# Attention beside an MLP on one core: one more add ahead of the logits in every chunk, a weight load in five parts, and a new order of pieces

## The chip, the cores and the metric

The kernel runs on one core of a Trainium2 chip. The metric is the device time of one execution in microseconds (us); the time given for a kernel is the median of its runs. Besides that there is one profiled execution of each kernel, from which all rows are taken.

## The reference

The layer norm of x (2048 tokens, 640 channels, bf16) goes through two branches, and both are added to x.

```python
xn  = layernorm(x)                                  # over 640 channels
q, k, v = split(xn @ wqkv)                          # 32 heads of 20 channels
idx = pos[:, None] - 2 * arange(8)[None, :]         # 8 keys, each 2 tokens further back
logits = einsum("hsd,hswd->hsw", q, k[idx]) * 20 ** -0.5      # idx < 0: -1e9
o   = einsum("hsw,hswd->hsd", softmax(logits), v[idx])
mlp = gelu(xn @ w1 + b1) @ w2 + b2                  # 640 -> 1536 -> 640
out = x + o @ wo + mlp
```

## The kernel before

Tokens are worked through in four chunks n = 0..3 of 512, and each chunk in four blocks of 128. The 640 channels make five tiles of 128 (KT = 5), with channels arranged so that the 128 partitions of a tile hold 4 channels of each of the 32 heads. An attention window of 8 keys is too small for matrix products over heads, so VectorE (DVE) does it: for each block j and half h of the window, qk multiplies q by four shifted views of k, [128, 4, 5, 128] in one instruction (L433), into the one buffer `half`.

The sum over a head's 20 channels is taken in two steps. First pa pieces on DVE add some channel tiles into others (L465, below). What is left is summed by lg on TensorE (PE): matmuls with `head_of`, a 128 x 32 matrix of zeros and ones, 128 x 512 columns each, the four blocks going to four groups of 32 columns (L474). `KEPT[n]` says how many channel tiles are left for lg: with 2, pa..0 adds tiles 2, 3 into 0, 1 (2048 elements a partition), pa..1 adds tile 1 into 0 (1024), and lg has 2 tiles x 2 halves x 4 blocks = 16 matmuls.

```python
a, b = ((slice(0, 2), slice(2, 4)), (slice(0, 1), slice(1, 2)), (slice(0, 1), slice(4, 5)))[k]
...
ts = {KT: range(KT), 3: (0, 1, 4), 2: (0, 4), 1: (0,)}[KEPT[n]]
...
for k in range({KT: 0, 3: 1, 2: 2, 1: 3}[KEPT[n]]):
    piece(f"pa{n}{j}{k}", do_pa, n, j, k)
```

Then come the softmax (cl copies the logits out of PSUM on ScalarE, ACT; m, mx, ss, ri, at on DVE; ex on ACT), xd (a DMA spreads the weights over the partitions), av (DVE multiplies v by them, into `half` again), aa (adds the two halves; a DMA of GpSimd's queue for chunks 0 to 2, DVE for chunk 3), ab and ot (the last adds on DVE, into the single buffer oT). Since `half` is there once, the order on DVE is qk, pa of chunk 0, then of chunk 1, av of 0, av of 1, qk of 2, and so on, and each hand-over waits for an lg.

PE has the other work: projections (hj for chunk 0, by pairs of blocks; pj for the others), the MLP's first product f1 with its Gelu ge on ACT, and the output products o{n}{block}{0..3} (MLP) and o{n}{block}4 (attention, which needs ot). Products of PE go to four PSUM banks that pieces share (psA), emptied by copies on ACT (pc, hc, gc) or by ge; outputs go to one pair lo, hi of banks, emptied by oc and stored by od with an adding DMA. ACT also does part of the layer norms (su, sq, rs, xn). Transposed x comes from PE in chunk 0 (tp, copied by tc), by DMA from SP's queue later (tc). xp stores x to the output, xb adds b2.

Each engine works its instructions off in order. That order is written by hand in ORDER, one string of piece names; a piece's engine and buffers are fixed, and its waits follow from what it reads and writes.

The first pieces: x's first block is loaded on SP's queue (L130), the second on ACT's; then SP loads wq, wk, two more blocks of x, wv, four more blocks of x, w1 in two parts, and (ldx) the rest of x. ga and gb2 to gb4 multiply block 0 by wq tile by tile of the inner 640 (ga: tiles 0 and 1, gb: 2, 3, 4; L349), gd and ge block 1; hj are L380, f1 L586, pj L336, o L622 and L624.

Of the kernel before, what the change touches and what calls it, by code (L numbers as in the profile page):

```python
# [39 lines left out]
ORDER = """  # L40
wa ho st00a sum1 st00 rs00 rc00 neg1 sq1 xn00a tp00a wb xn00b tp00b mean1 tc00a rs01 rc01 tb b1 tc00b ga gb2 xn01 tp01
tc01a tc01b gb3 gb4 gd ge gc4 gc1 hj100 st02a st02 rs02 hc100 st03a st03 hj101 gc0 rc02 xn02 rs03 hj102 rc03 xn03
hc101 hc102 tp02 tc02 hj202 tp03 tc03 hj201 hc201 hj010 st11a hc010 st13a hc202 st12a hj012 hc012 hj112 hc112 f10_3
st11 ldx hj011 f10_9 st10a st10 st12 st13 rs1 qk011 ge0_3 rc1 xn13 pad01 qk000 qk001 tc13 ge0_9 xn12 tc12 pa000 qk010
pk hj110 hc110 hj111 hc111 hc011 qk030 qk031 qk021 pad11 xn11 f10_10 tc11 pa010 xn10 qk020 tc10 ge0_10 f10_2 ge0_2
hj200 hc200 f10_0 pa030 f10_6 f10_11 su20 ge0_6 xp2 su22 su23 pj111 pc111 ge0_0 su21 ng2 pj110 pc110 pj104 pc104 sq23
pj120 pc120 ge0_11 sq20 pj114 pc114 pj113 pc113 pa001 pa020 pa021 pj102 pc102 pa031 pa011 lg0 cl0 mask m0 hj212 hc212
pj123 pc123 mx0 ex0 pj103 pc103 pj112 pc112 ss0 ri0 pj101 pc101 pj100 pc100 qk110 qk100 ld2 ldo xb2 sq22 qk130 pj124
pc124 hj211 sq21 qk121 rs2 pj121 pc121 hj210 hc210 rc2 f10_8 qk131 hc211 f11_9 ge1_9 xp0 xn20 f10_1 ge0_1 f10_7 tc20
f11_5 xb0 qk120 xn21 tc21 qk101 ge1_5 ge0_7 xn23 tc23 ge0_8 xn22 qk111 o000 f11_8 ge1_8 pa130 at0 pa110 f11_0 ge1_0  # L50
pa100 pad12 f10_5 ge0_5 f11_3 ge1_3 f11_6 su32 tc22 pa120 pa101 xd00 f10_4 su33 pj214 pc214 pa111 su31 su30 pj210
pc210 pad21 xd02 ge0_4 pj211 pa121 ge1_6 pa131 lg1 pj200 pad02 av000 av001 aa00 pc200 ng3 sq32 sq31 sq30 av020 pc211
av021 xd01 av011 o001 pj213 pc213 pj122 pj202 pc202 av010 o002 ab00 ot00 pj204 pj212 o003 pc212 pj223 pj222 cl1 aa02
xd03 pc122 av030 av031 m1 mx1 sq33 rs3 pj201 rc3 pc204 o004 oc00 ab02 ot02 pj224 ex1 o020 aa01 aa03 ss1 ri1 xn33 at1
ab01 ot01 ab03 o021 o022 o023 o024 xp1 tc33 pc201 xn32 tc32 pc222 oc02 ot03 od02 f12_7 xd10 av101 pad22 xd12 pc223
f11_4 xn30 o030 o031 o032 o033 pc224 xd11 xn31 pj221 av100 aa10 o034 oc03 f11_2 o010 ge1_4 tc31 av120 o011 o012 o013
o014 av110 av111 aa11 ge2_7 pc221 od03 f11_7 ge1_7 pj203 pc203 ge1_2 xd13 f11_1 av131 tc30 pj311 pc311 av130 aa13
pj304 f12_3 ge2_3 pj310 pc310 pc304 ge1_1 pj302 av121 aa12 ab10 ot10 f11_10 pc302 ge1_10 pj313 pc313 qk201 qk200 pj312
pj314 ab11 ot11 qk210 pc312 oc01 od01 f13_8 ge3_8 qk211 o130 ab13 pa200 pc314 f11_11 ge1_11 qk231 f12_6 o131 ot13
qk230 xb3 f12_0 ge2_0 pj220 pc220 o132 o133 o134 oc13 pj301 pc301 pa210 ge2_6 ab12 ot12 qk221 pj300 pj324 pc300 qk220  # L60
f13_7 xb1 pc324 od13 pa211 pj303 o120 pa230 pa220 pa231 pc303 pad31 pa221 pa201 lg2 ge3_7 cl2 qk301 f12_2 m2 mx2 ex2
f13_10 f12_8 ge2_8 o121 o122 o123 od00 o124 oc12 qk310 ss2 pj320 pc320 qk311 ri2 at2 xd22 xd20 o110 o111 qk331 o112
o113 o114 oc11 od11 qk330 f13_6 ge3_6 f12_5 ge2_5 ge3_10 o100 ge2_2 qk320 pa330 qk321 pa320 f13_5 f12_4 ge3_5 pj322
f13_2 o101 ge2_4 qk300 xd21 pc322 pa321 o102 o103 o104 ge3_2 pa300 pa301 pa331 pa310 pa311 lg3 f13_3 av210 f13_9 oc10
od10 od12 av211 aa21 ge3_3 f12_10 ge2_10 xd23 av230 av200 f12_1 ge2_1 ge3_9 av231 aa23 f12_9 ge2_9 f13_1 ge3_1 f13_4
f12_11 av201 av221 ab21 ge3_4 av220 pj321 o210 o211 o212 f13_0 ot21 ge2_11 o213 o214 f13_11 cl3 m3 mx3 ex3 pad32 ss3
ri3 at3 xd32 oc21 o200 o201 pc321 o202 aa20 ab20 ot20 ab23 ot23 ge3_0 aa22 o203 o310 o204 oc20 pj323 pc323 ab22 ot22
av320 o230 o231 o232 o233 o234 od20 oc23 av321 aa32 xd30 o311 o312 od21 ab32 o220 o221 o222 o223 o224 ge3_11 xd31
av311 od23 o313 av301 av310 oc22 od22 o320 o321 o322 o323 av300 ot32 o324 oc32 aa31 ab31 ot31 o314 oc31 o300 o301 o302
xd33 od32 aa30 o330 o303 ab30 ot30 o304 av331 av330 aa33 ab33 o331 o332 o333 ot33 od31 xl o334 oclo oc30 ohi ochi ochd  # L70
od30
""".split()


# [713 lines left out]
```

## Time and profile before

| | us |
|---|---|
| runs | 206.86, 207.37, 207.10; median 207.1 |
| profiled execution, own time | 207.49 |
| its span in the profile | 205.7 |
| PE busy | 200.8 |
| DVE busy | 175.4 |
| ACT busy | 127.7 |

The granted clock is 1.0. A row of the profile names the source line, the engine, the operation, what it writes and reads, the shape, how often it ran, its busy time and its mean. A row of a timeline begins with the start and the length of a merged run of equal instructions; in square brackets stands how long the engine was idle ahead of it and what ended that. The chain of waits lists, in order of time, the work that ended last, followed back from the end. Neighbouring instructions overlap by some 0.1 us on DVE and by more on PE, so what an instruction costs in a run is the distance to the next start, not its length.

### The profile page before, as it was taken

What the parts mean: (1) busy time and instruction counts of PE and PEld (TensorE: products, weight loads), DVE (VectorE), ACT (ScalarE), POOL (GpSimd) and SP (SyncE); (2) the same over time, 40 slices, a digit from 0 to 9 for tenths busy, and PEclk for the clock granted to TensorE, in tenths of its full rate; (3) what the DMA queues carried; (4) which work ended last, traced back from release to release, by engine and by line L of the source; (5) the groups of instructions that cost most, each with busy time, mean ns of one, the idle gap of its engine ahead of it and who ended that gap; (6) DMA issues with size and microseconds to landing.
All of it is one profiled execution on the core that took longest, in us unless ns stands there. A gap on an engine that the chain in (4) does not pass through costs nothing.

```text
span 205.7 us, 3262 instructions
## 1 busy us (share of the span) xinstructions
PE 200.8 (98%) x1285; PEld 112.2 (55%) x1285; DVE 175.4 (85%) x214; ACT 127.7 (62%) x242; POOL 34.4 (17%) x49
## 2 busy tenths in 40 slices
PE   7899999999999999999999999999999999999994
PEld 2797745565445555555555554555444555555552
DVE  3489999379998989949999994999979979799981
ACT  5488999899999879916466344834616854221210
POOL 2000000050000422102703303001023420311210
DMA  6999389969258599899996965018209998931244
GB/s 210 390 397 370 75 232 326 403 102 185 64 116 264 99 186 181 142 192 124 207 198 113 144 107 64 0 16 182 41 0 132 162 193 162 192 41 17 30 52 64
DMA packets 27335, 31.77 MB, mean 154 GB/s; under 512 B 9272, under 2 KB 22072, under 8 KB 27320
## 3 DMA queue, kind: packets, MB, share of 16 engines
q0 software_dynamic: 7408, 12.78, 39.4%
q1 hardware_dynamic: 19600, 18.58, 31.4%
q8 instruction: 10, 0.16, 0.3%
q10 hardware_dynamic: 312, 0.20, 0.3%
q14 instruction: 5, 0.04, 0.1%
HBM read 10.00 MB, written 7.54 MB: 85 GB/s over the span
## 4 chain that ended last, share of the span: by engine, by line
PE 95%; DMA 3%; SPq 0%; DVE 0%; issue 0%
PE lo L622 29%; PE hps L586 25%; PE pps L336 24%; PE hi L624 7%; PE gps L380 7%; DMA wq_sb<-in_A_wqkv_dram 3%; PE L L474 2%; PE gps L349 1%; PE tp L280 0%; SPq L130 0%; DVE osb L652 0%
## 5 line engine op out<-in xcount | busy, mean ns | idle before, releaser
L586 PE MATMUL hps<-xnT,w_sb 128*128 128x512 bf16 x240 | 55.6, 379 | 0.0
L433 DVE TENSOR_TENSOR half<-qT,kT 128x2560 bf16<-128x2560 bf16 x32 | 46.2, 1482 | 2.9 <-PE L L474 2.8
L622 PE MATMUL lo<-w_sb,hT 128*128 128x512 bf16 x144 | 41.3, 379 | 0.0
L586 PEld LDWEIGHTS <-w_sb 128*128 128x128 bf16 x240 | 22.9, 98 | 26.3 <-issue 0.8
L629 ACT CAST osb<-lo 128x512 bf16<-128x512 f32 x15 | 8.8, 587 | 36.8 <-PE hi L624 18.5
L624 PE MATMUL hi<-w_sb,hT 128*128 128x128 bf16 x144 | 31.5, 219 | 0.0
L602 ACT ACTIVATE hT<-hps,b1T 128x512 bf16<-128x512 f32 x36 | 24.0, 683 | 10.7 <-PE hps L586 10.7
L465 DVE TENSOR_TENSOR half<-half 128x2048 bf16<-128x2048 bf16 (+1 forms) x32 | 29.0, 952 | 0.2
L635 POOL DMA_DIRECT2D out_dram<-osb x15 | 13.6, 973 | 77.1 <-ACT osb L630 68.5
L557 DVE TENSOR_TENSOR half<-vT,x_sb 128x2560 bf16<-128x2560 bf16 x16 | 22.8, 1485 | 4.4 <-DMA x_sb<-e 3.0
L557 DVE TENSOR_TENSOR half<-vT,ax 128x2560 bf16<-128x2560 bf16 x16 | 22.8, 1485 | 2.3 <-PE L L474 1.4
L622 PEld LDWEIGHTS <-hT 128*128 128x128 bf16 x144 | 14.1, 98 | 16.8
L622 PE MATMUL lo<-wo,oT 128*128 128x512 bf16 x80 | 23.1, 379 | 0.0
L567 POOL DMA_DIRECT2D half<-half x12 | 14.3, 1195 | 48.9 <-DVE half L557 48.5
L336 PE MATMUL pps<-xnT,wv_sb 128*128 128x512 bf16 x75 | 18.5, 379 | 0.0
L336 PE MATMUL pps<-xnT,wq_sb 128*128 128x512 bf16 x75 | 18.3, 379 | 0.0
L336 PE MATMUL pps<-xnT,wk_sb 128*128 128x512 bf16 x75 | 17.7, 379 | 0.0
L624 PE MATMUL hi<-wo,oT 128*128 128x128 bf16 x80 | 16.9, 219 | 0.0
L173 ACT ACT_TABLE_LOAD x12 | 15.4, 1283 | 0.9 <-PEq L772 0.7
L624 PEld LDWEIGHTS <-hT 128*128 128x128 bf16 x144 | 14.1, 98 | 2.2
L573 DVE TENSOR_TENSOR half<-half 128x1280 bf16<-128x1280 bf16 x16 | 13.1, 820 | 1.3 <-DMA half<-half 1.2
L622 PEld LDWEIGHTS <-oT 128*128 128x128 bf16 x80 | 7.8, 98 | 9.4
(91 smaller groups left out, 263.7 us busy)
## 6 DMA issues: line engine op xcount, KB each, us to landing
half<-half POOLq DMA_DIRECT2D x12, 640.0 KB, 7.1
w_sb<-in_B_w_dram SPq DMA_DIRECT2D x4, 960.0 KB, 11.0
out_dram<-osb POOLq DMA_DIRECT2D x15, 160.0 KB, 4.0
ax<-e SPq DMA_DIRECT2D x8, 256.0 KB, 4.8
x_sb<-e SPq DMA_DIRECT2D x8, 256.0 KB, 4.8
out_dram<-b2bc POOLq DMA_DIRECT2D x3, 640.0 KB, 8.7
x_sb<-in_A_x_dram SPq DMA_DIRECT2D x1, 1280.0 KB, 12.9
out_dram<-x_sb SPq DMA_DIRECT2D x2, 640.0 KB, 8.7
```

The lines of the kernel that those rows point to most:

```text
L173: nc.scalar.activation(warm[:], nc.const_aps.tensor(0.0, [P, 1], F32), func)
L336: nc.tensor.matmul(ps[:], lhsT=wqkv_p[which][:, ti, to, :], rhs=xnT[:, ti, :], start=(ti == 0), stop=(ti == KT - 1),)
L380: nc.tensor.matmul(ps[:, to - a, :], lhsT=wqkv_p[which][:, ti, to, :], rhs=tiles["xnT", 0][:, ti, pair * 2 * P : (pair + 1) * 2 * P], star ...
L433: nc.vector.tensor_tensor(out=half[:, j, h], in0=q[:, :, at].unsqueeze(1).to_broadcast([P, W // 2, KT, P]), in1=window(k, h, at), op=ALU.mult,
L465: nc.vector.tensor_tensor(out=kept, in0=kept, in1=gone, op=ALU.add)
L557: nc.vector.tensor_tensor(out=half[:, j, h], in0=window(qkv_tile(n, 2), h, cs), in1=ax_view(n)[:, j, ws, :].unsqueeze(2).to_broadcast([P, ...
L567: nc.gpsimd.dma_start(a, b, accum_op=ALU.add, max_dma_last_dim=CUT)
L586: nc.tensor.matmul(ps[:], lhsT=w1_sb[:, ti, ft * P : (ft + 1) * P], rhs=tiles["xnT", n][:, ti, :], start=(ti == 0), stop=(ti == KT - 1),)
L602: nc.scalar.activation(hT, tiles["hps", n, ft][:], ACT.Gelu_apprx_tanh, bias=b1T[:, ft : ft + 1], scale=1.0)
L622: nc.tensor.matmul(lo[:], lhsT=lhs, rhs=rhs[:, 0:CH], start=first, stop=last)
L624: nc.tensor.matmul(hi[:, 0 : D - CH], lhsT=lhs, rhs=rhs[:, CH:D], start=first, stop=last)
L635: nc.gpsimd.dma_start(rows, tiles["osb", n, bl][:], accum_op=ALU.add)
```

## The change

`KEPT` is 1 for all chunks. So each block has a third add, pa..2, of tile 4 into tile 0 (16 more instructions on DVE, 1024 elements a partition), and each lg has 8 matmuls, over tile 0 alone (32 fewer in all). wq comes in five DMAs, one for each tile of the inner dimension, 160 KB each, in place of one of 800 KB. ORDER is new throughout. The core of the diff, with a part of the two orders:

```diff
-KEPT = (2, 2, 2, 2)
+KEPT = (1, 1, 1, 1)
...
-wa ho st00a sum1 st00 rs00 rc00 neg1 sq1 xn00a tp00a wb xn00b tp00b mean1 tc00a rs01 rc01 tb b1 tc00b ga gb2 xn01 tp01
-tc01a tc01b gb3 gb4 gd ge gc4 gc1 hj100 st02a st02 rs02 hc100 st03a st03 hj101 gc0 rc02 xn02 rs03 hj102 rc03 xn03
-hc101 hc102 tp02 tc02 hj202 tp03 tc03 hj201 hc201 hj010 st11a hc010 st13a hc202 st12a hj012 hc012 hj112 hc112 f10_3
...
+sum1 neg1 wb ho wa st00a st00 rs00 sq1 mean1 rc00 xn00a tp00a xn00b tp00b rs01 tc00a ldx ga tc00b rc01 xn01 tp01 tc01b
+tb b1 tc01a gb2 gb3 gb4 st02a st02 gc0 st03a hj100 hc100 rs02 rc02 gd ge hj101 st03 rs03 gc1 xn02 rc03 gc4 tp02 tc02
+xn03 tp03 tc03 hj202 hc202 hc101 hj102 hc102 pk st12a hj012 st12 hc012 hj011 hc011 st13a st13 st10a hj111 hc111 hj110
+st11a st11 pad01 st10 qk011 rs1 rc1 f10_3 ge0_3 qk010 xn12 hj112 hc112 hc110 qk000 tc12 xn13 tc13 hj201 pa010 hj212
+hc212 hj010 hc010 qk031 hc201 qk030 pa011 f10_9 qk021 qk001 ge0_9 xn11 tc11 pa012 f10_10 ge0_10 xn10 f10_2 ge0_2 f10_0
...
+pj120 pc114 pc120 pa020 pj102 pc102 sq22 sq20 pj111 pa001 pa021 pc111 pa002 pa022 pj110 pc110 pj113 pc113 pj101 pa032
+sq21 lg0 cl0 pj104 pc104 mask m0 ld2 mx0 pj112 ex0 xp0 ldo xb0 pc101 pj103 pc103 ss0 ri0 pj100 pc100 pc112 qk121 hj210
...
+ge0_4 su32 pa112 xp1 pa101 pj202 pc202 pj214 pc214 pj211 pj213 pa122 su31 pc213 su33 pa102 ng3 pad12 o001 pa132 lg1
+cl1 xd00 pc211 pj204 pj122 pc204 pad02 pc122 av000 sq32 av001 aa00 m1 av020 pj212 pc212 sq30 pj210 pc210 pj220 ge1_8
...
+o002 o003 o004 oc00 od00 ss1 ri1 at1 sq31 pj221 pc221 xd10 pc220 rs3 rc3 xn33 tc33 ab01 ot01 ab03 ot03 o020 av101 xd13
...
+pc300 qk221 pad31 o130 o131 o132 o133 o134 od01 qk220 pa211 oc13 pj304 pa220 pa231 pa221 pc304 o120 pa212 o121 pa222
+pa232 lg2 pc312 qk300 qk321 od02 cl2 m2 qk330 f12_10 o122 o123 o124 oc12 qk301 qk311 f12_11 ge3_7 ge2_10 f13_5 ge2_11
...
+ge2_5 pa312 pa330 oc10 od10 f12_8 ge2_8 pa321 pa331 pa322 f12_4 pa332 lg3 xd23 av210 av211 f13_1 ge3_1 f13_10 ge3_10
...
+pc323 f13_4 ge3_4 m3 mx3 ab21 ot21 av221 av220 ex3 ss3 ri3 at3 pj321 o213 o214 o310 xd30 aa20 ab20 ot20 oc21 ab23 ot23
+o311 o200 pc321 o201 o202 pad32 o331 av301 o203 o204 oc20 f13_11 aa22 ab22 ge3_11 o230 o231 o232 od20 xd32 av321 xd31
...
+ot30 o304 oc30 av331 od30 aa33 ab33 ot33 xl o332 o333 o334 oclo ohi ochi ochd
...
-    load_w(0)
+    for a in range(5):
+        ks = slice(a * KT // 5, (a + 1) * KT // 5)
+        nc.sync.dma_start(wqkv[0][:, ks, :], wqkv_v[:, ks, 0:D])
     load_w(1)
```

Before, the four hand-overs stood in ORDER as `pa031 pa011 lg0 cl0 mask`, `pa131 lg1`, `o120 lg2` (behind `pa221 pa201`) and `pa310 pa311 lg3`.

More of the change, by code (lines that the diff above doesn't have):

```diff
@@ L40 @@
 ORDER = """
-wa ho st00a sum1 st00 rs00 rc00 neg1 sq1 xn00a tp00a wb xn00b tp00b mean1 tc00a rs01 rc01 tb b1 tc00b ga gb2 xn01 tp01
-tc01a tc01b gb3 gb4 gd ge gc4 gc1 hj100 st02a st02 rs02 hc100 st03a st03 hj101 gc0 rc02 xn02 rs03 hj102 rc03 xn03
-hc101 hc102 tp02 tc02 hj202 tp03 tc03 hj201 hc201 hj010 st11a hc010 st13a hc202 st12a hj012 hc012 hj112 hc112 f10_3
-st11 ldx hj011 f10_9 st10a st10 st12 st13 rs1 qk011 ge0_3 rc1 xn13 pad01 qk000 qk001 tc13 ge0_9 xn12 tc12 pa000 qk010
-pk hj110 hc110 hj111 hc111 hc011 qk030 qk031 qk021 pad11 xn11 f10_10 tc11 pa010 xn10 qk020 tc10 ge0_10 f10_2 ge0_2
@@ L46 @@
[L46 to L70, printed above, removed]
@@ L71 @@
-od30
+sum1 neg1 wb ho wa st00a st00 rs00 sq1 mean1 rc00 xn00a tp00a xn00b tp00b rs01 tc00a ldx ga tc00b rc01 xn01 tp01 tc01b
[3 more added lines that the diff above has]
+hc212 hj010 hc010 qk031 hc201 qk030 pa011 f10_9 qk021 qk001 ge0_9 xn11 tc11 pa012 f10_10 ge0_10 xn10 f10_2 ge0_2 f10_0
@@ new lines @@
+ge0_0 su20 pa030 f10_6 ge0_6 hj200 su23 qk020 f10_11 su21 ge0_11 su22 tc10 pj123 hc200 pc123 pa000 ng2 pa031 pj114
+pj120 pc114 pc120 pa020 pj102 pc102 sq22 sq20 pj111 pa001 pa021 pc111 pa002 pa022 pj110 pc110 pj113 pc113 pj101 pa032
+sq21 lg0 cl0 pj104 pc104 mask m0 ld2 mx0 pj112 ex0 xp0 ldo xb0 pc101 pj103 pc103 ss0 ri0 pj100 pc100 pc112 qk121 hj210
+qk130 hc210 qk111 pj121 f11_6 sq23 rs2 rc2 qk120 xp2 pc121 at0 hj211 hc211 f10_1 ge0_1 pa120 qk131 qk110 xn21 tc21
+pad11 qk101 pa130 pj124 f10_7 ge0_7 o000 xn20 f10_5 ge0_5 ge1_6 pc124 f10_8 ge0_8 tc20 f11_8 xd01 xn22 pa110 tc22 xn23
@@ new lines @@
+tc23 xd02 f11_3 ge1_3 qk100 pa111 pa100 f11_9 pad21 ge1_9 su30 f10_4 f11_0 f11_5 ge1_0 ge1_5 pa131 pj200 pc200 pa121
+ge0_4 su32 pa112 xp1 pa101 pj202 pc202 pj214 pc214 pj211 pj213 pa122 su31 pc213 su33 pa102 ng3 pad12 o001 pa132 lg1
+cl1 xd00 pc211 pj204 pj122 pc204 pad02 pc122 av000 sq32 av001 aa00 m1 av020 pj212 pc212 sq30 pj210 pc210 pj220 ge1_8
+av021 aa02 pj222 pj201 pc201 av011 av010 mx1 pj203 pc203 ab00 ot00 xd03 av030 av031 f12_3 aa01 ex1 ab02 ot02 aa03 sq33
+o002 o003 o004 oc00 od00 ss1 ri1 at1 sq31 pj221 pc221 xd10 pc220 rs3 rc3 xn33 tc33 ab01 ot01 ab03 ot03 o020 av101 xd13
@@ new lines @@
+o021 o022 o023 o024 oc02 xn31 xd11 av100 av131 av111 f11_4 pj224 pc224 pc222 av130 o030 o031 xn30 o032 o033 o034 oc03
+tc31 f11_7 o010 f11_1 xd12 av121 o011 o012 ge1_1 o013 o014 aa10 ge1_4 av110 av120 tc30 ge1_7 ab10 xn32 pad22 ot10
+qk201 qk200 pa200 ge2_3 pa201 aa11 aa13 od03 f12_0 ge2_0 f12_6 ge2_6 pj223 tc32 f11_10 ge1_10 ab11 pj312 pc223 pj314
+pc314 pj301 pc301 f12_7 ge2_7 pj302 qk211 ot11 f11_11 ge1_11 pj311 pc311 pj313 pc313 pc302 pa202 f13_8 qk210 ab13
+f11_2 ge1_2 pa210 pj310 ge3_8 pc310 f13_7 ot13 qk231 qk230 aa12 ab12 xb1 pj303 pc303 pa230 oc01 pj324 pc324 ot12 pj300
@@ new lines @@
+pc300 qk221 pad31 o130 o131 o132 o133 o134 od01 qk220 pa211 oc13 pj304 pa220 pa231 pa221 pc304 o120 pa212 o121 pa222
+pa232 lg2 pc312 qk300 qk321 od02 cl2 m2 qk330 f12_10 o122 o123 o124 oc12 qk301 qk311 f12_11 ge3_7 ge2_10 f13_5 ge2_11
+qk331 ge3_5 mx2 ex2 qk310 ss2 pj322 pj320 pc320 pa310 qk320 pc322 o110 f12_2 od12 ri2 at2 xd21 xd22 o111 o112 od13 xb2
+o113 o114 oc11 od11 pa300 pa320 f13_2 ge3_2 o100 o101 pa301 f13_6 o102 o103 ge2_2 pa311 o104 f13_3 ge3_3 pa302 f12_5
+ge2_5 pa312 pa330 oc10 od10 f12_8 ge2_8 pa321 pa331 pa322 f12_4 pa332 lg3 xd23 av210 av211 f13_1 ge3_1 f13_10 ge3_10
@@ new lines @@
+av230 f12_9 av231 xd20 av201 av200 f13_0 ge3_6 f12_1 ge2_9 ge2_1 pj323 o210 ge2_4 o211 o212 aa21 cl3 ge3_0 o330 aa23
+pc323 f13_4 ge3_4 m3 mx3 ab21 ot21 av221 av220 ex3 ss3 ri3 at3 pj321 o213 o214 o310 xd30 aa20 ab20 ot20 oc21 ab23 ot23
+o311 o200 pc321 o201 o202 pad32 o331 av301 o203 o204 oc20 f13_11 aa22 ab22 ge3_11 o230 o231 o232 od20 xd32 av321 xd31
+ot22 av320 av310 aa32 od21 av311 aa31 av300 xd33 o233 o234 oc23 o312 ab32 o220 o221 o222 o223 o224 oc22 xb3 od22 f13_9
+ab31 o320 o321 ge3_9 o313 od23 o322 ot32 o323 o324 oc32 od32 ot31 o314 aa30 av330 o300 o301 o302 o303 oc31 od31 ab30
```

## The prediction

> **What bounds the kernel now.** I read the page's first two parts, then the chain of waits in order of time, then DVE's timeline, then the issues on SP.
>
> ```profile
> PE 200.8 (98%) x1285; PEld 112.2 (55%) x1285; DVE 175.4 (85%) x214; ACT 127.7 (62%) x242; POOL 34.4 (17%) x49
> PE 95%; DMA 3%; SPq 0%; DVE 0%; issue 0%
> ```
>
> PE is busy 98% of the span and 95% of the chain is PE. The chain itself:
>
> ```profile
> 1.20 5.51 DMA wq_sb<-in_A_wqkv_dram
> 6.76 1.03 PE gps L349 x15
> ...
> 36.60 0.98 PE L L474 x16
> ...
> 63.92 1.07 PE L L474 x16
> ...
> 127.06 0.98 PE L L474 x16
> ...
> 151.97 0.98 PE L L474 x16
> ...
> 202.00 0.96 PE hi L624 x17
> ```
>
> From 6.76 to 202.96 us PE has no hole. So a piece starts at 6.36 us plus the PE work ahead of it (1.08 for an f1 or pj, 1.36 for an o..4, 0.815 for the other o pieces; the sum gives 126.7 for lg2, which the chain has at 127.06). I call 6.36 PE's lag. Only PE work taken away, or a hole put in, moves the end. DVE does have holes:
>
> ```profile
> 38.70 0.21 DVE L490 TENSOR_TENSOR Lb<-Lb,mask 32x128 bf16<-32x128 bf16 x1 [2.57 <-ACT Lb L486]
> 42.45 0.69 DVE L519 TENSOR_TENSOR sums<-e 128x512 f32<-128x512 bf16 x1 [1.77 <-ACT e L513]
> ...
> 90.58 11.30 DVE L557 TENSOR_TENSOR half<-vT,x_sb 128x2560 bf16<-128x2560 bf16 x8 [3.01 <-DMA x_sb<-e]
> ...
> 120.53 4.76 DVE L465 TENSOR_TENSOR half<-half 128x1024 bf16<-128x1024 bf16 x6
> 128.12 1.49 DVE L433 TENSOR_TENSOR half<-qT,kT 128x2560 bf16<-128x2560 bf16 x1 [2.83 <-PE L L474]
> ...
> 198.79 0.49 DVE L577 TENSOR_TENSOR oT<-half 128x640 bf16<-128x640 bf16 x1
> ```
>
> From the first qk (17.40) to the last ot (199.28) its holes add up to 16.5 us; that is the room for new DVE work. o334 starts at 200.92, so DVE is 1.64 early at the end.
>
> **PE work removed.** Each lg has 8 matmuls instead of 16. Sixteen take 0.98 to 1.07: four run side by side on four column groups, so a round is some 0.22 (o pieces: 0.22 to the next) and four rounds are 0.87 plus 0.1 to 0.2 of start. Two rounds: 0.55 to 0.6. The saving is 0.43 (a round's price twice) to 0.49 (half), not below nothing since no matmul is added. I take 0.44: **-1.75** over four chunks.
>
> **DVE work added.** Sixteen adds of 128x1024. The page has that form at 684 ns; in the run of six above (two of 128x2048, which take 1.14 to the next start, four of 128x1024) one takes 0.60 to the next start when it doesn't wait for its forerunner, and 0.66 in the run at 146.36 where it does. Bounds 0.55 (684 less the 0.1 to 0.13 by which neighbours overlap) to 0.72; I take 0.64: 10.2 us, 2.56 a chunk. All of it must go into the 16.5 us of holes. Which holes stay is read from the new order.
>
> **The first 14 us.** wq in five loads of 160 KB: x's first load has that size and landed 2.5 us after its issue, so the first two parts are there by some 5 us and ga waits for tc00a only. neg1 now stands ahead of rs00 on ACT (0.18 later): tc00a ends at 6.25 instead of 6.05, ga starts at 6.30: -0.46. SP spends five issues of some 0.42 where it spent one. wk, x's next blocks, wv and w1 are all issued 1.7 later, and in the built program each also waits for an earlier load (wk for x's first block, then wq's parts), so a late one holds every issue behind it. I cost that at nothing: by the windows the DMA share is 1.01 to 1.08 from 3 to 20 us, so landings follow the bytes queued ahead, and 160 KB per 0.42 feeds 380 GB/s where 385 to 397 are moved. If that cover is gone, x's third load (13.37) and the first qk slip by up to 1.7. tp01 waits 0.1 for xn01. hj100 comes forward, ahead of gd, to 8.16 (6.30, 25 gps at 1.95 / 35 = 0.056, tp01 and tb 0.34, the 0.1), and wk landed at 8.8 (1.67 + 7.1): hole 0.65. tp03 now has only hj101 and tp02 ahead of it and waits for xn03 (13.1 as before, since x's load of two blocks, issued at 2.23, lands only 7.3 later): PE is there at 12.7 (8.8, twice 1.09, 25 gps, tp02), hole 0.45. Sum -0.46 + 1.2: **+0.75**, PE's lag is 7.13.
>
> **DVE against PE, join by join.** Each stretch is laid out piece by piece in the new order. Prices on PE: two-tile hj 1.09, one-tile 0.545, f1 and pj 1.08, o as above, lg 0.5 here. On DVE, by the distance to the next start: qk and av 1.405, pa..0 1.14, other pa 0.64, ab 0.84, ot 0.42, m 1.04, mx 0.62, ss 1.5, ri 0.93, at 0.62, rc 0.29, aa of chunk 3 1.5. PE's work ahead of lg0 is 6.3 (up to tp03), 5 one-tile and 6 two-tile hj and 15 f1 or pj: 31.77; to lg1 lg0, 22 f1 or pj, 2 hj and 2 o more: 59.84; to lg2 lg1, 34, 20 o and 5 o..4: 120.16; to lg3 lg2, 12, 10 and 3: 145.85; to o334 192.09.
> - qk031 is reached at 23.05 (17.4 with 3 qk, rc1, pa010) and needs hc010, on ACT behind the Gelu table load, ge0_3, xn12, hc112, hc110, xn13 and hc212: 23.75. DVE hole 0.7. Then pa032 ends at 39.35 (8 qk, rc, 4 and 8 pa since 17.4). PE reaches lg0 at 31.77 + 7.13 = 38.9: hole **0.35**.
> - cl0, mask: DVE hole 1.6 (2.57 before); ex0 behind its table load: 1.1 (1.77 before). pc101 now stands behind ex0 (43.95) on ACT, and hj210 needs the bank that pc101 empties: PE hole **0.4**. tc23 is in at 61.5, when PE wants it: **0.1**.
> - From qk121 (46.45) DVE runs through 8 qk, rc, at, 4 and 8 pa: pa132 ends at 68.3. PE reaches lg1 at 59.84 + 7.95 = 67.8: hole **0.45**. av000 follows at 68.5, 0.2 behind pa132; xd00, now issued behind xp1 at some 62, is in by then.
> - at1 ends at 86.95 (8 av, 2 ab, 2 ot, m to at). xd10 took 5.2 from its issue (85.35) to the multiplication at 90.58. The adds between are done by 89.8: hole 2.4 (3.01 before), av101 at 92.2.
> - pa232 ends at 129.4 (8 av, 4 ab, 4 ot, 8 qk, 12 pa), PE reaches lg2 at 128.6: hole **0.7** (lg2's first matmuls, on tiles already done, run ahead). pa332 ends at 155.05 (8 qk, 12 pa, m to at), lg3 is reached at 154.95: **0.1**, and 0.2 on DVE ahead of av210.
> - m3 and ss3 have multiplications in front and don't wait (1.12 before). at3 ends at 172.4 (8 av, ab, ot, m to at); xd30 again 5.1, covered for 2.5: hole 2.6. The last ot ends at 201.05 (8 av, 4 aa, 5 ab, 5 ot) and o334 is reached at 192.09 + 9.2 = 201.3. The same sums over the kernel before come out 0.9 short for DVE at its last ot and 0.47 short for PE at its end: with those, 201.95 against 201.75, hole **0.2**.
>
> DVE's holes come to 8.8: of the 10.2 us added, 7.7 are paid from waits that shrink, the rest makes the holes on PE. PE: -1.75 + 0.75 + 0.35 + 0.4 + 0.1 + 0.45 + 0.7 + 0.1 + 0.2 = **+1.3**. On the profiled execution (span 205.7, with 1.8 around it 207.49) that is 208.8. It lay 0.39 above the median of the runs, 207.1: **208.4**. The work behind ot33 (o334, ohi, the last store) is unchanged.
>
> **Rivals.**
> *Faster: the joins are met.* If an add costs 0.55, DVE is 0.36 earlier at lg0 and that much more at each lg, and the holes at the four lg's and o334 (1.8) go; if wk lands 0.65 sooner, that one goes too. 1.3 - 2.45 is -1.15: **206.0**. For it: the overlap of neighbours in DVE's timeline. Against: pa..1 and pa..2 of one j both wait for pa..0, and the DMA queue is full until 20 us.
> *Slower: DVE becomes the bound.* With 0.72 an add (+1.3) and one of the two xd landings at the 6.2 that is the longest for x_sb<-e (+1.2), the last ot ends 2.5 later, at 204.45, and o334 (1.08) and ohi (0.96) follow: 206.5 against 202.96, +3.5: **210.6**. It decides from a last ot later than 201.75, where my sum already stands. For it: all five joins above meet within 0.9 us, and a slip of either engine costs PE, while an early arrival earns nothing. Against: the median landing is 4.8.
> *The matmuls bring nothing.* If eight cost as much as sixteen (a fixed cost per switch to the 32-column tile), +1.75: **210.1**. The chain's 0.98 for sixteen leaves little room.
> *The small loads run one after the other.* Five times x's 2.5 us would bring wq at 13.7 instead of 6.7, gb4 and all behind it some 5 us later, of which about 4 reach lg0: **212.4**. Against: three loads were in flight at 4 us, at 387 GB/s. The Trainium skill ("DMA: Bandwidth & Descriptors", section "Bandwidth") rules to batch loads to 1 MiB or more for 75% of the peak, which speaks against the five. By the sum in its section on the anatomy of one DMA (2.0 us and the bytes at 436 GB/s) a 160 KB load would take 2.4, an estimate; five in a row 11.9, and the kernel would come out near 211.8. This trace's windows (387 GB/s with a 160 KB load and an 800 KB load in flight) speak for loads that overlap.
>
> **Chances and range.** The bound for "same" is 0.3% (0.6 us): the three runs before spread by 0.25%. Forecast 0.50, its own range 207.2 to 209.6 (lg -0.2; adds between 0.60 and 0.68 give 0.6 each way at the later joins; wk 0.4); faster rival 0.23; DVE the bound 0.19; matmuls 0.04; loads 0.04. Of the forecast 0.11 lies between 206.5 and 207.7, and 0.02 of the faster rival. That is 0.21 faster, 0.13 same, 0.66 slower. The range goes down to 205.7 (the faster rival with 0.3 more from the first 14 us) and up to 211.0; it leaves out the loads and the far ends of the others.
>
> **What would show it.** In the profile after: L474 x8 at 0.55 to 0.6 in the chain; the first gps at 6.3 and a hole on wk_sb near 8.2; DVE busy some 11 us more; PE holes of 0.3 to 0.8 ahead of the first three lg's and almost none at the end. Wrong: PE holes of over 1.5 us together after 150 us (DVE is the bound), a wq part landing after 8 us, or no hole at the lg's.

## The result, and the profile after

The changed kernel takes 219.7 us (median of six runs, 218.1 to 221.4) against 207.3 (206.9 to 207.4): ratio 1.059, 95% interval 1.053 to 1.065. The ratio leaves out the run of 221.4, which lies over 1.5% above the fastest. The forecast was 208.4, its range ended at 211.0. The sign was right, the size was not: 12.5 us lost where 1.3 were foreseen. The profiled execution took 220.3, with a span of 218.3.

The page's engine row, its row of granted clocks, and the chain's shares by engine:

```profile
PE 203.8 (93%) x1231; PEld 113.2 (52%) x1253; DVE 184.1 (84%) x230; ACT 127.4 (58%) x242; POOL 34.6 (16%) x49
PEclk9969999999979999999999999999999999999999
PE 50%; DVE 21%; DMA 10%; issue 10%; ACT 4%; POOL 1%; SPq 1%; DVEq 0%; ACTq 0%; POOLq 0%
```

PE carries half of the chain instead of 95%, and PE's granted clock, which was full all through, has two dips (the 6 and the 7 in the second row). The chain of waits (start, length, what):

```profile
3.57 7.30 DMA wk_sb<-in_A_wqkv_dram
10.91 2.18 PE gps L382 x10
13.09 2.15 PE gps L351 x25
...
42.52 0.55 PE L L476 x8
...
60.26 0.25 ACT kT L409
...
76.95 0.33 PE L L476
...
114.16 0.84 DVE half L575
...
139.87 0.59 PE L L476 x5
...
165.74 0.55 PE L L476 x8
...
213.76 0.96 PE hi L626 x17
```

Eight matmuls of an lg take 0.55, as forecast. I call a piece's start minus the PE work ahead of it PE's lag, as the prediction does (with its own sums: 31.77, 59.84, 145.85 and 193.17 ahead of lg0, lg1, lg3 and ohi). It comes to 10.7, 17.1, 19.9 and 20.6; forecast were 7.5, 8.4, 9.2 and 9.4. So of the 11.2 us too much, 3.3 are lost by lg0, 5.4 more between lg0 and lg1, 2.0 by lg3, 0.5 at the end. Some 0.5 of this is no loss: by that much the prediction's sums are short at PE's end for the kernel before too.

**By lg0.** SP's issues, and PE's timeline:

```profile
1.21 2.31 SPq L141 DMA_DIRECT2D wq_sb<-in_A_wqkv_dram  x5
3.57 0.44 SPq L133 DMA_DIRECT2D wk_sb<-in_A_wqkv_dram  x1
10.91 2.18 PE L382 MATMUL gps<-xnT,wk_sb 128*128 128x256 bf16 x10 [2.65 <-DMA wk_sb<-in_A_wqkv_dram]
12.88 2.36 PE L351 MATMUL gps<-xnT,wq_sb 128*128 128x128 bf16 x25
```

wk, issued at 3.57 instead of 1.67, lands 7.3 us later, as it did before (7.1), so 2.0 later on the clock. The cover on which the prediction relied, a DMA queue so full that later issues cost nothing, is not there. In windows of one microsecond (busy times of PE, PEld, DVE, ACT and POOL, granted clock, DMA share, GB/s), first before, then after:

```profile
4.00:5.00 1.00, 0.65 (x6) 0.32 (x4) 0.54 (x3) 0.93 (x5) 0.00 (x0) 1.00 1.04 386
5.00:6.00 1.00, 0.57 (x8) 0.40 (x8) 0.94 (x4) 0.97 (x3) 0.00 (x0) 1.00 1.05 374
```

```profile
4.00:5.00 1.00, 1.00 (x9) 0.58 (x7) 0.59 (x4) 0.97 (x5) 0.00 (x0) 1.00 0.71 164
5.00:6.00 1.00, 0.68 (x9) 0.33 (x6) 0.87 (x4) 0.97 (x3) 0.00 (x0) 1.00 0.93 321
```

Five issues of 160 KB (163,840 bytes) take 2.36 us up to the next issue and so feed 347 GB/s, less than was moved before, and in the window from 4 to 5 us the rate falls to 164. The bytes are not the whole of it: by 9 us 2.13 MB were moved where it had been 2.58, which at 390 GB/s is an estimated 1.1 us of the 2.0. And the wait is not all of the loss: hj100's ten matmuls take 2.18 us where they took 1.09. Two windows behind the hole:

```profile
10.90:13.00 2.10, 2.09 (x12) 1.55 (x13) 1.26 (x4) 0.00 (x0) 0.00 (x0) 0.56 1.06 389
13.00:15.20 2.20, 2.20 (x28) 2.20 (x27) 1.37 (x6) 1.07 (x3) 0.00 (x0) 0.65 1.06 399
```

At 0.56 and 0.65 these 4.3 us held 2.6 us of full-speed work: 1.7 us lost (2.10 x 0.44 + 2.20 x 0.35), on top of the hole. The hole is 2.0 longer than forecast, and the forecast wait of 0.45 for xn03 did not come: 2.0 + 1.7 - 0.45 is the 3.3 that are lost by lg0.

**Between lg0 and lg1.** One copy on ACT, the piece pad11, and PE's next group:

```profile
60.26 0.25 ACT L409 COPY kT<-kT 128x70 bf16<-128x70 bf16 x1 [4.09 <-DVE half L435]
61.15 1.97 PE L588 MATMUL hps<-xnT,w_sb 128*128 128x512 bf16 x6 [3.63 <-ACT hT L604]
63.00:66.00 3.00, 2.78 (x8) 1.08 (x8) 3.00 (x4) 2.74 (x5) 0.00 (x0) 0.54 0.66 128
```

pad11 writes the first columns of chunk 1's kT. In the old ORDER it stands ahead of all multiplications qk that read that tile; in the new one behind six of them ("qk131 qk110 xn21 tc21 pad11"), and it waits for the last. ACT works in order, so ge0_7 waits behind it. ge0_7 would have emptied the PSUM bank that PE needs next; PE stands 3.6 us, and then again loses 1.7 to the clock. DVE, which was to be what lg1 waits for, is done early and stands 5.7 us ahead of av000:

```profile
77.37 2.89 DVE L559 TENSOR_TENSOR half<-vT,ax 128x2560 bf16<-128x2560 bf16 x2 [5.71 <-PE L L476]
```

**Later.** PE stands 1.0 us at pj312 near 114 and 1.6 us in lg2, whose matmuls wait one by one for DVE. DVE had waited for DMAs before that:

```profile
100.38 7.13 DVE L559 TENSOR_TENSOR half<-vT,x_sb 128x2560 bf16<-128x2560 bf16 x5 [1.24 <-DMA x_sb<-e]
108.07 4.30 DVE L559 TENSOR_TENSOR half<-vT,x_sb 128x2560 bf16<-128x2560 bf16 x3 [0.56 <-DMA x_sb<-e]
114.16 0.82 DVE L575 TENSOR_TENSOR half<-half 128x1280 bf16<-128x1280 bf16 x1 [1.80 <-DMA half<-half]
```

### The profile page after: what moved, and what is told of

Read it like the earlier page. It is cut to its first block, busy times and chain, and to the rows that moved or that the text cites. A ratio compares the mean times of both kernels' runs of the same rounds, so it can differ in the third digit from the quotient of the medians.

```text
span 218.3 us, 3194 instructions
## 1 busy us (share of the span) xinstructions
PE 203.8 (93%) x1231; PEld 113.2 (52%) x1253; DVE 184.1 (84%) x230; ACT 127.4 (58%) x242; POOL 34.6 (16%) x49
## 4 chain that ended last, share of the span: by engine, by line
PE 50%; DVE 21%; DMA 10%; issue 10%; ACT 4%; POOL 1%; SPq 1%; DVEq 0%; ACTq 0%; POOLq 0%
PE hps L588 16%; PE lo L624 14%; DVE half L435 9%; PE pps L338 9%; PE gps L382 6%; DMA half<-half 5%; DVE half L467 5%; PE hi L626 4%; DVE half L559 4%; DMA wk_sb<-in_A_wqkv_dram 3%; DMA out_dram<-osb 2%; DVE half L575 1%; PE gps L351 1%; SPq L141 1%; ACT qT L402 1%
## 5 line engine op out<-in xcount | busy, mean ns | idle before, releaser
L588 PE MATMUL hps<-xnT,w_sb 128*128 128x512 bf16 x233 | 57.6, 386 | 4.3 <-ACT hT L604 3.6
L624 PE MATMUL lo<-w_sb,hT 128*128 128x512 bf16 x139 | 40.3, 379 | 0.4 <-ACT osb L631 0.4
L467 DVE TENSOR_TENSOR half<-half 128x1024 bf16<-128x1024 bf16 (+1 forms) x48 | 38.7, 862 | 0.1
L631 ACT CAST osb<-lo 128x512 bf16<-128x512 f32 x15 | 8.8, 584 | 33.6 <-PE hi L626 12.5
L569 POOL DMA_DIRECT2D half<-half x12 | 15.3, 1350 | 68.4 <-DVE half L559 68.4
L637 POOL DMA_DIRECT2D out_dram<-osb x15 | 14.7, 1070 | 66.3 <-ACT osb L632 66.3
L307 POOL DMA_DIRECT2D out_dram<-b2bc x4 | 8.6, 2150 | 43.4 <-DMA b2bc<-in_B_b_dram 43.4
```

Source lines behind the costliest of these rows:

```text
L467: nc.vector.tensor_tensor(out=kept, in0=kept, in1=gone, op=ALU.add)
L569: nc.gpsimd.dma_start(a, b, accum_op=ALU.add, max_dma_last_dim=CUT)
L588: nc.tensor.matmul(ps[:], lhsT=w1_sb[:, ti, ft * P : (ft + 1) * P], rhs=tiles["xnT", n][:, ti, :], start=(ti == 0), stop=(ti == KT - 1),)
L624: nc.tensor.matmul(lo[:], lhsT=lhs, rhs=rhs[:, 0:CH], start=first, stop=last)
L637: nc.gpsimd.dma_start(rows, tiles["osb", n, bl][:], accum_op=ALU.add)
```

## The experiments

Theory A: the loss is a few waits of the new order and the five loads, made larger by the clock. The rival: DVE with its sixteen additions is the bound. All ratios are to runs of the kernel before that were taken alongside.

### The two large holes

**wq in one DMA (e1)**, the rest as changed:

```
-    for a in range(5): ... nc.sync.dma_start(wqkv[0][:, ks, :], wqkv_v[:, ks, 0:D])
+    load_w(0)
```

> The changed kernel with wq's weights in one DMA again; order and additions unchanged. Theory A (the five issues put wk's issue 1.9 us later on SP, the PE hole on wk_sb grows from the forecast 0.65 to 2.65 us, and the granted clock of 0.53 and 0.65 behind it costs some 1.8 more): wk lands near 8.8, x's third load near 9.6, first qk near 17.5, PE's lag behind tp03 7.1 instead of 10.7, and the kernel is 3 to 4 us faster than the changed one's 219.7: 216 to 217. Rival (DVE is the bound, so an earlier PE earns little): less than 1.5 us gained, 218.3 or more.

218.3 us, ratio 1.053 (1.049 to 1.057): only 1.5 us won. By its total that is the rival's number, not theory A's. But the start did what theory A says: hj100 at 8.13 without a wait, first qk at 16.7, lg0 at 38.20 instead of 42.45. Later a PE hole of 2.7 ends at pj312 (1.0 in the changed kernel), with a slow clock behind it:

```profile
112.71 4.01 PE L336 MATMUL pps<-xnT,wk_sb 128*128 128x512 bf16 x10 [2.69 <-DMA xnT<-xn]
```

The 4.2 us won are mostly given back there, in a wait for a DMA and not for DVE's additions.

**pad11 early (e2)**, ahead of xn11; ORDER only:

```
- ... qk131 qk110 xn21 tc21 pad11 qk101 ...
+ ... qk021 qk001 ge0_9 pad11 xn11 ...   (and no pad11 ahead of qk101)
```

> The changed kernel with one ACT copy moved: pad11 ahead of xn11, in front of all multiplications qk of chunk 1, as it stood before. Theory A (pad11 waits 4.1 us for DVE's qk110 and holds ge0_7, xn20 and what follows on ACT; PE stands 3.6 us and then runs at a granted clock of 0.54 to 0.83): the hole on hT near 57 goes, lg1 starts near 71.5 instead of 76.9, and the time falls by 5 to 6.5 us, to 213.2 to 214.7. Rival (DVE is the bound: with its sixteen more additions it could not have been at lg1 earlier): less than 2 us gained, 217.7 or more, with PE waiting at lg1 for DVE's half instead.

214.3 us, ratio 1.034 (1.028 to 1.039): 5.4 us won. In PE's timeline lg1 starts at 71.09 instead of 76.88:

```profile
71.09 0.69 PE L476 MATMUL L<-half,head_of 128*32 128x512 bf16 x8
```

DVE's last addition ends at 71.1, so the two just meet there; DVE was not in the way, and the rival is wrong for lg1.

**Both edits (e3):**

> Both edits: wq in one DMA and pad11 early; the sixteen additions, the eight-matmul lg's and the rest of the new order stay. Theory A: the two gains add up, 8.5 to 10 us, 209.5 to 211.5, within 3 us of the forecast 208.4; what is left above it are waits for DVE at lg2 and for DMAs near 194. Rival (DVE is the bound): 214 or more, with DVE without holes and PE waiting at every lg.

Four runs: 207.9, 211.6, 211.9 and 214.6, too far apart for a ratio; their mean granted clocks are 1.000, 0.992, 0.992 and 0.984 in the same order. The profiled one is the slowest. PE's timeline and a window of it:

```profile
107.32 4.43 PE L336 MATMUL pps<-xnT,wk_sb 128*128 128x512 bf16 x10 [3.09 <-DMA xnT<-xn]
107.30:112.80 5.50, 5.48 (x13) 1.97 (x14) 5.33 (x6) 0.59 (x1) 1.28 (x1) 0.50 1.10 207
```

A third place: chunk 3's last transpose (tc32) lands 8.2 us after its issue, PE waits 3.1 us for it, and 5.5 us at half clock behind the wait cost 2.7 more.

**The clock by itself (e4):** eleven matmuls on constants, ahead of hj100, in the hole of the changed kernel.

```
+ for _ in range(11): nc.tensor.matmul(spare[..., 0:CH], lhsT=ones[:, 0:P], rhs=ones[:], start=True, stop=True)
- ... gc0 st03a hj100 ...
+ ... gc0 st03a wf hj100 ...
```

> The changed kernel with eleven extra matmuls of 128x512 on constants, ahead of hj100, in the 2.65 us in which PE waits for wk (they add nothing to the output). Theory A (PE's clock is lowered because PE stood idle): the granted clock stays near 1.0 from 8 to 16 us, hj100 takes 1.1 instead of 2.18 and the 25 matmuls of chunk 1's q 1.4 instead of 2.15; 1 to 1.8 us gained: 218 to 218.7. Rival (the clock is lowered for another reason, such as the many transfers in flight at the start): rows and time as in the changed kernel, 219.7 or later.

218.9 us, ratio 1.057 (1.053 to 1.061), 0.8 us better, where at least 1 was expected. PE's timeline and windows:

```profile
8.26 2.57 PE L459 MATMUL spare<-const-bfloat16-1.0 128*128 128x512 bf16 x10
10.66 1.25 PE L382 MATMUL gps<-xnT,wk_sb 128*128 128x256 bf16 x10
10.90:13.00 2.10, 2.10 (x33) 2.10 (x31) 1.51 (x6) 0.78 (x2) 0.00 (x0) 1.00 1.06 394
13.00:15.20 2.20, 2.20 (x29) 2.07 (x27) 2.08 (x7) 1.52 (x4) 0.00 (x0) 1.00 1.07 401
```

The clock stays at 1.00 with as many transfers in flight (394 to 401 GB/s): in the changed kernel it fell because PE stood idle. lg0 is reached 1.9 us earlier (40.52); of this, pj312's hole takes a part again (1.8 instead of 1.0).

### Each part of the change in the old order

**The additions and short lg's alone (e6)**, in the kernel before:

```
- KEPT = (2, 2, 2, 2)
+ KEPT = (1, 1, 1, 1)      (ORDER: each pa..2 right behind its pa..1 or pa..0, whichever is later)
```

> The kernel before with the additions alone: KEPT at 1 for all chunks, each pa..2 right behind its pa..1 or pa..0, the old order otherwise, wq in one DMA. Theory A (an addition costs where DVE and PE meet): in the old order DVE's last addition ends 0.4, 0, 1.7 and 0.5 us ahead of the need at the four lg's, against 2.56 us added at each; DVE is 10.2 later less 2.6 of slack, less 1.75 of shorter lg's on its path and 1.6 at the end: 4 to 5 us slower, 211 to 212.5, with PE holes of 1 to 2.5 us ahead of lg's. Rival 1 (DVE's 16.5 us of holes take the additions in any order): 206.5 or less. Rival 2 (the holes on PE also lower the clock): 213 or more.

217.1 us, ratio 1.049 (1.044 to 1.053): rival 2. PE waits for DVE at lg's, the clock falls twice (1.7 us lost each time), and DVE and PE share the chain 53% to 35%:

```profile
39.28 0.61 PE L474 MATMUL L<-half,head_of 128*32 128x512 bf16 x7 [2.18 <-DVE half L465]
69.08 0.38 PE L474 MATMUL L<-half,head_of 128*32 128x512 bf16 x1 [0.84 <-DVE half L465]
70.41 0.59 PE L474 MATMUL L<-half,head_of 128*32 128x512 bf16 x5 [0.95 <-DVE half L465]
41.20:43.20 2.00, 2.00 (x6) 0.73 (x5) 1.65 (x5) 0.76 (x3) 1.44 (x1) 0.50 0.30 110
```

So the additions are no gift: without a new order they cost 10 us.

**The five loads alone (e7)**, in the kernel before:

```
- load_w(0)
+ for a in range(5): ... nc.sync.dma_start(wqkv[0][:, ks, :], wqkv_v[:, ks, 0:D])
```

> The kernel before with the five wq DMAs alone, the old order and KEPT 2. Theory A (five issues put off everything behind them on SP by some 1.9 us, with no cover): wk issued at 3.6 and landed at 10.9 (before 1.7 and 8.8), PE waits 0.6 to 1 us for it, x's third load lands at 11.7 (9.6), first qk near 19.5 (17.4): 208.2 to 209.8. Rival (the queue is full anyway, as the prediction took it): landings as before, 206.6 to 207.5.

209.5 us, ratio 1.011 (1.006 to 1.015): 2.35 us by the medians, as expected in size, but not by the expected way in the profiled run (208.75). There wk landed 5.7 us after its issue and PE, with gd and ge still ahead of hj100, did not wait for it; what was late is x, with 0.57 us of PE's time ahead of a transpose and the first qk at 17.93. ohi starts 0.45 later than before (202.45), and from the last DVE add to the end it is 0.85 longer (3.56 us, before 2.71). So 0.45 is the start's in that run; the other three runs have no profile.

**wk issued by ACT (e11)**, in the kernel with pad11 early and five loads:

```
- load_w(1)
+ nc.scalar.dma_start(wqkv[1][:], wqkv_v[:, :, D : 2 * D])      (behind b1's load)
```

> The changed kernel with pad11 early (214.3), wq still in five DMAs, but wk's load issued by ACT behind b1's instead of by SP behind the five. Theory A (wk is late because it is issued late): wk lands near 8.8, PE waits for it 0.7 us or less instead of 2.7, the clock stays near 1.0 behind it; x's third load is still late (11.2, its issue comes only 0.4 us sooner), so DVE's first qk stays near 19.3 and lg0 comes near 40 instead of 42.3: 2 to 2.5 us faster, 211.8 to 212.3. Rival (the queues are full and landings follow the bytes): wk lands at 10 or later, 213.8 or more.

A miss: 217.0 us, 2.7 worse. wk was issued at 0.73, ahead of b1's load and of x's second block, though it is written behind them, and PE no longer waited for it. But ACT came to b1's load only at 5.55 and to its first table load, behind that, at 6.15 instead of 0.74:

```profile
6.15 1.28 ACT L175 ACT_TABLE_LOAD   x1 [6.15 <-DMA wk_sb<-in_A_wqkv_dram]
```

sum1, first on ACT in the new order, began at 7.55 instead of 3.52, with rs00 behind it, and the first transpose came at 9.41 instead of 5.40, after 3.9 us without PE work and at half clock. So the run does not test what wk's late issue costs; it only shows that a load goes early when issued early.

### What was left

**pj312 later (e5)**, on top of the two mended places:

```
- ... ab11 pj312 pc223 pj314 pc314 pj301 pc301 f12_7 ge2_7 pj302 ... f11_11 ge1_11 ... f11_2 ge1_2 ...
+ ... ab11 pc223 f12_7 ge2_7 f11_11 ge1_11 f11_2 ge1_2 pj312 pj314 ...
```

> The last kernel (wq in one DMA, pad11 early) with three f1 and their Gelus (f12_7, f11_11, f11_2) ahead of pj312 instead of behind it, so that the first piece that needs the last transpose of chunk 3 (tc32) stands 3.2 us later on PE; the additions stay. Theory A: the third place where time went is that transpose, which landed 8.5 us after xn32 was done; in the profiled run with 214.6 PE stood 3.1 us on xnT there and then had a granted clock of 0.50 for 5.5 us, and the run of 207.9, whose mean clock was 1.0, had no such hole. Now no run has it: median 207.5 to 208.7, runs within 1 us, mean clock 1.0. Rival (something else spreads the runs): median 211 or more, runs 4 us apart as before.

213.5 us, ratio 1.029 (1.023 to 1.036): a miss for the total, which is the rival's. The hole at pj312 is gone, but a hole of 3.2 us in lg2 takes its place. DVE's timeline says why:

```profile
105.66 0.83 DVE L573 TENSOR_TENSOR half<-half 128x1280 bf16<-128x1280 bf16 x1 [2.18 <-DMA half<-half]
```

ab10 waits for aa10, the first DMA addition of chunk 1, issued at 94.69 and landed 10.9 us later, with the transposes tc30 and tc32 under way (SP, 94.68 to 100.9).

**The same with KEPT at 2 (e8)**, pa..2 left out: the new order without additions:

> The first kernel of this set (wq in one DMA, pad11 early, pj312 later) with KEPT at 2, the sixteen additions left out: the new order alone. By the prediction's terms the additions are worth -1.75 on PE and +1.8 in holes at the joins, so nothing in sum: within 0.7 us of the first kernel, 207.3 to 208.9. Rival (DVE is the bound with the additions): 1.5 us or more faster than the first kernel. Rival (the shorter lg's come free): 1 us or more slower.

211.0 us, ratio 1.017 (1.013 to 1.020): 2.5 us faster than with the additions, which the rival had said. The additions cost something in this order too, beyond the 1.75 that they save. In its profiled run, the slowest of the four (213.1), lg2 still waits (1.5 us) behind ab10's wait (2.8).

**Chunk 3's statistics early (e9)**, on top of e5, with all additions:

```
- ... aa01 ex1 ab02 ot02 aa03 sq33 ... ss1 ri1 at1 sq31 ... xd10 pc220 rs3 rc3 xn33 tc33 ... xn31 ... tc31
+ ... sq33 sq31 pc201 ... aa01 rs3 ex1 ab02 ot02 aa03 ... rc3 xn33 xn31 ss1 tc33 ri1 at1 ... tc31 xd10
```

> The kernel with wq in one DMA, pad11 early and pj312 later, and chunk 3's statistics and first transposes earlier: sq33 and sq31 ahead of pc201, rs3 ahead of ex1 (as in the old order), xn33 and xn31 ahead of at1, tc33 and tc31 ahead of xd10. Theory A: what is left there is DVE's wait of 2.2 us in ab10 for the DMA addition aa10, which took 10.9 us because two transposes of chunk 3 (tc30, tc32) were under way beside it, and it comes out at lg2 as a PE hole of 3.2 us. With the transposes out of the way aa10 takes 8 to 9 us, DVE waits less than 0.6 us in ab10, the hole at lg2 is 1 us or less: 2 to 3.5 us faster than without the edit (213.5): 209.5 to 211.5, and the span of an undisturbed run near 207. Rival (lg2's hole is DVE's load of additions): aa10 faster or not, lg2's hole stays over 2 us, 212.5 or more.

209.5 us, ratio 1.011 (1.008 to 1.013), four runs within 0.4 us, clock 1.0 in each. DVE's timeline around ab10, and lg2:

```profile
92.91 11.30 DVE L557 TENSOR_TENSOR half<-vT,x_sb 128x2560 bf16<-128x2560 bf16 x8 [3.17 <-DMA x_sb<-e]
104.14 0.82 DVE L573 TENSOR_TENSOR half<-half 128x1280 bf16<-128x1280 bf16 x1
129.84 0.59 PE L474 MATMUL L<-half,head_of 128*32 128x512 bf16 x5 [0.22 <-DVE half L465]
```

ab10 does not wait any more, and lg2's hole is 1.7 (2.23 from its start to the next piece's, where 0.55 is needed); 1 or less was expected. DVE's last addition ends at 129.8, 0.4 later than the prediction laid out, and PE is there at 128.13, 0.5 earlier. PE's lag at lg0, lg1 and lg3 is 6.8, 7.5 and 9.8, where the forecast, with the five loads, had 7.5, 8.4 and 9.2.

**The same with chunk 2's additions left out (e10)**, `KEPT = (1, 1, 2, 1)`:

> The same kernel with chunk 2's additions left out (KEPT 1, 1, 2, 1): 2.56 us less on DVE ahead of lg2, 0.44 more on PE. Theory A (lg2's hole is under 1 us by now): 0 to 0.5 us faster than the kernel with all additions. Rival (DVE's additions are what PE waits for at lg2): 1.5 us or more faster.

208.4 us, ratio 1.004 (1.003 to 1.006): 1.15 us faster, nearer to the rival. lg2 has no hole in its profiled run (0.98 from 128.33 to the next piece). The hole at lg2 is DVE's load: four additions cost more there than the 0.44 they save.

**The whole change but for the three places in the order (e13)**, that is e9 with wq in five DMAs again:

> The kernel with all sixteen additions and the three mended places (pad11 early, pj312 later, chunk 3's statistics early; 209.5), now with wq in five DMAs again: the whole change but for those places. Theory A (the start costs the hole on wk and the lowered clock behind it): wk lands near 10.9, PE stands 2.6 us, the clock is near 0.5 for some 3 us, lg0 comes 3.7 to 4.2 us later than with one DMA (38.5), and DVE's first qk 2.2 us later takes nothing off that: 213.2 to 213.7. Rival (in this order only the 2.35 us that the five DMAs cost in the kernel before): 211.6 to 212.2.

213.3 us, ratio 1.029 (1.026 to 1.032), 3.8 more than with one load: theory A's price. It is a median of unlike runs, 1.7 to 4.4 above e9's. In the profiled one (211.25) wk came 6.3 us after its issue, PE waited 1.5 us, and the clock stayed full; two of the others (213.6 and 213.9) have a mean clock of 0.992, as one dip gives.

By the medians, then, the 12.5 us divide into 6.4 for the three places in the order, pad11, pj312 and chunk 3's statistics (changed kernel to e13), 3.8 for the five loads (e13 to e9) and 2.3 that are left (e9 to the kernel before).

**Versions meant to be faster.** The first (e12), from e9:

```
- KEPT = (1, 1, 1, 1)
+ KEPT = (1, 2, 2, 1)
- ... tc10 pj123 ... cl0 pj104 pc104 mask ... xb0 pc101 pj103 ... hc211 f10_1 ge0_1 pa120 ... xn21 ...
+ ... tc10 f10_1 ge0_1 pj123 ... cl0 pj104 pc104 pc101 mask ... xb0 pj103 ... hc211 pa120 ... xn21 ...
```

> A candidate for the best version: wq in one DMA, pad11 early, pj312 later, chunk 3's statistics early, KEPT at (1, 2, 2, 1) so that DVE is early at lg1 and lg2, pc101 on ACT ahead of ex0 (it stood behind it and held hj210's bank, a PE hole of 0.4) and f10_1 ahead of pj123 (which waited for chunk 1's last transpose). By PE's account: 205.7 of span, less 0.88 for two shorter lg's, and 0.4 to 1 us of holes at the start and at lg0: 206.8 to 207.8, no change or a little faster than before (207.2). Rival (the new order is in itself worse by over 1 us somewhere not yet seen): 208.2 or more.

211.4 us, ratio 1.018 (1.015 to 1.021): a miss. With ge0_1 gone from ahead of xn21, ACT went into xn21's wait for DVE (1.55 us) before it loaded its Gelu table, and PE stood 1.9 us. Two more, with pc101's move and without f10_1's: KEPT at (1, 1, 2, 1) (e14) and at (1, 2, 2, 1) (e15).

> The kernel with KEPT at (1, 1, 2, 1) and the mended places (208.4), with pc101 on ACT ahead of ex0 and nothing else moved. Theory A (hj210 waits for the bank that pc101 empties, 0.4 us, as the prediction had it, and DVE is at lg1 just when PE is): the PE hole at hj210 goes, and most of it comes back as a longer hole at lg1: 0 to 0.4 us faster, 208.0 to 208.4. Rival (PE is late everywhere behind hj210): 0.4 us faster or more.

> The same with KEPT at (1, 2, 2, 1): chunk 1's additions left out too, 2.56 us less on DVE ahead of lg1 against 0.44 more on PE. Unlike the candidate before it (211.4), f10_1 and ge0_1 stay where they are, ahead of xn21 (with ge0_1 gone from there, ACT went into xn21's wait for DVE ahead of its Gelu table load, and PE stood 1.9 us). Theory A (DVE is what PE waits for at lg1): 207.0 to 207.9. Rival (PE is late from the start): 208.2 to 208.8.

208.7 (ratio 1.007, 1.005 to 1.009) and 208.8 (1.008, 1.006 to 1.010). hj210's hole goes and comes back as 0.6 us in lg1. With chunk 1's additions left out that goes too, but the time does not fall, which is the rival's outcome; in its profiled run, the slowest of six (209.7), PE waits 1.7 us near 184. None beats the kernel before, and what keeps the last 1.2 us (e10) stays open.

## Why the prediction was wrong

- **The first 14 us: +0.75 forecast.** PE's lag was to be 7.5 at lg0 and came to 10.7; the five loads alone are 3.8 us of the time (e13 against e9). The step that failed is "I cost that at nothing", the 1.7 us of issues on SP. It set 160 KB per 0.42 against the bytes moved (380 GB/s); an issue takes 0.47 with its gap (347 GB/s), so wk's comes 1.9 later, and the window of 4 to 5 us fell from 386 to 164 GB/s. The text gave "If that cover is gone" 1.7 us for x (the first qk did slip, by 2.3 to 19.68), but left wk at 8.8 in the same breath; with hj100 brought ahead of gd it is wk that decides. What sets wk's landing stays open: with the same five loads it came 7.3 us after its issue here, 5.7 in e7 and 6.3 in e13. ga's gain (start 6.16 instead of 6.76) and the early wq parts (landed 2.8 to 4.1 us after issue) were right. Small loads one after another did not come true; the 2.4 us a load that the prediction takes for them from the Trainium skill is stated there for DMAs issued by GpSimd, and these were issued by SP.
- **What no step had: the clock.** The sum prices a hole at its length. The holes on wk and pad11 cost 1.7 us more each, that on tc32 in e3 2.7. For the hole on wk e4 shows that the idle PE is the cause.
- **What no step had: pad11.** The join at lg1, with a forecast hole of 0.45, was laid out on DVE and PE only, and that is the costliest error of the layout. A copy of 0.25 us on ACT that had changed sides with the qk of its tile cost 5.4 us (e2).
- **lg2, 0.7 forecast:** 1.6 in the changed kernel and 1.7 with the other places mended. The additions are 0.61 us each (38.7 against 29.0 us busy, over 16), under the 0.64 taken, but ab10's wait for aa10 (1.8 in the changed kernel) was in no sum. With that wait gone (e9) the hole stays, since PE, with one load, is there earlier than forecast and DVE is not. The layout also took pj312 for granted, and tc32 was not followed.
- **Right:** the lg's 0.55; the additions' price; hj210 0.4 (0.37 measured); mask 1.6 and ex0 1.1 (1.89 and 1.22); av301 2.6 (2.48). With the places mended and one load the forecast's 208.4 was missed by 1.1 (e9), or by 1.9 without the 0.75 that it counts for the five loads. The joins are where the additions cost: e6 and e10 show it.
- **The signs it named.** lg0 and lg1 start without a hole, since PE comes later than DVE, and DVE is busy 8.7 us more (184.1 against 175.4) where 11 were named. Two small slips: at lg0 its own two times (39.35 and 38.9) differ by 0.45, not by the 0.35 that it counts, and between 3 and 4 us the kernel before moved 328 GB/s, not 385 or more.
- **"The work behind ot33 is unchanged"** was wrong as well: from the last DVE add to the end it is 3.55 us instead of 2.71. In every profile with the five loads it is 3.5 or more, with the old order too (e7, 3.56); with one load it is 2.7 in the old order (e6 too) and 3.1 to 3.25 in the new. The last store lands 1.5 us after its issue both before and after, so the 0.8 lies behind that landing; what it is stays open.
- **The rival "DVE becomes the bound"** (210.6) was not what happened in the changed kernel; it is what happens to the additions without the new order (e6), and at lg2 in part with it (e10).

## What to carry to other kernels

When an order is rewritten, follow every moved piece on every engine, the cheap copies too: ask of each which readers of its tile it has changed sides with, and what stands behind it in its queue. A load split in parts can cost its issues to all that the same queue issues later, and here a busy DMA queue did not hide that; compare the bytes per issue with the bytes moved, and ask what waits for the later loads. And look at the granted clock behind a PE hole: in these runs each single hole of 2.65 us or more cost 1.5 to 3.0 us beyond its length.

## What the runs showed of the hardware

The granted clock fell to 0.50 with each single PE idle time of 2.65 us or more (2.65, 2.7, 2.9, 3.1, 3.6, 3.9), after two in a row of 0.84 and 0.95 with single matmuls between (e6, lg1) and after one of 2.18 (e6, lg0), but not after 1.5 (e13), 1.9 (e12) or 2.04 (e6, lg3). Summed over its windows, one dip costs 1.7 us, that is 3.4 us at half clock, in the changed kernel (twice), in e1 (twice), e2 and e4, and at both of e6's dips; in e3 and e11 it is twice that (3.4 us lost, 6.8 at half clock). In e2, e3 and e11 the dip begins within the idle time, so that part of it costs nothing. The Trainium skill ("TensorE: Matmul & The Clock Gate", section "Part 1: The HAM clock gate") states such a clock, half-rate after an idle window of some 3.4 us and full again after a busy one, with windows that run freely; the length of the dips agrees, while idle times from 2.2 us on were enough here.

Issuing an 800 KB load as five cost SP 2.3 us instead of 0.4 (L141 x5 against L133). The Trainium skill ("DMA: Bandwidth & Descriptors", section "Issuing engines are not separate DMA queues") calls the time to initiate a DMA usually small beside the DMA itself; the trace agrees if the DMA is taken from issue to landing (0.46 against 2.8 to 4.1), but not against the bytes alone, an estimated 0.42 us for 160 KB at the 390 GB/s of the windows.

An addition by DMA of 640 KB (aa10) took 8.3 to 12.6 us in the eight profiles in which both transposes tc30 and tc32 were issued beside it (the changed kernel, e1 to e5, e8 and e11), and 6.1 to 6.6 in the six in which tc30 went out 3.5 us or more ahead of it (e9, e10 and e12 to e15). Transposes are not all: in each of these profiles a later addition took 12.8 us or more.
